# Windowed attention with sinks and a maxout FFN: 32-wide TensorE tiles for the sink part, output banks by head pair, and a split last output

## The chip, the cores and the metric

The kernel runs on one core of a Trainium2 chip. The core has TensorE (PE in the profile; PEld are its weight loads), VectorE (DVE), ScalarE (ACT), GpSimd (POOL) and SyncE (SP), which here only issues DMAs. The metric is the device time of one execution in microseconds; the time of a kernel is the median of its runs.

## The reference

Attention over 4 batches, 8 heads, 768 tokens, head size 64. A token sees itself and the 127 before it, and the first four tokens of its sequence (the sinks). The result, heads side by side, goes through an FFN whose hidden layer is the maximum of three products.

```python
scores = scale * np.matmul(q, k.transpose(0, 1, 3, 2))
is_sink = pos[None, :] < 4
in_window = (rel >= 0) & (rel < 128)              # rel = query position - key position
a = softmax(np.where(is_sink | in_window, scores, -1e9))
x = np.matmul(a, v)                               # -> (B*S, H*D) = (3072, 512)
h = np.maximum(np.maximum(x @ w1, x @ w2), x @ w3)    # d_ff = 768
return h @ w_out                                  # (3072, 512), float32
```

## The kernel before

Work is cut into 12 chunks of 256 tokens (`NCH`), three to a batch (`CPB`). In the first chunk of a batch (0, 3, 6, 9) the sinks are ordinary keys of the chunk's own blocks. In the other eight (1, 2, 4, 5, 7, 8, 10, 11) the sinks lie in front of the window and have matmuls of their own. A chunk has two halves of 128 tokens (`t`), and its heads come in four pairs (`p`, `NP`), 128 rows of d for each pair.

The order is written out by hand: `manual_schedule` keeps each engine in the order of the program, and strings such as `"Fa3 Ab00 Fa4"` list the steps. The first letter is the step, the second the chunk (a, b, c ... are given with the call), the rest its argument:

- K, Q: transposes of k and q on TensorE (`prep`, the first four chunks); D: the same by a DMA transpose on SP (`turn`), and E copies k into its place (`place_k`).
- L loads q, k and v of a chunk on SP's queue; `cast` turns them into bf16, mostly on POOL.
- S: window scores, two matmuls with 64 rows each per pair, and their exponentials on ACT (L271, L277); B only opens the banks. M: the mask, a product on DVE (L284).
- Z: sink scores (`sink_score`, L290), four matmuls that add up in one bank, and one exponential into `e_sink` (L295). Row 8·s + head of that bank holds the score of sink s for the head; `ks` carries the four sink keys, spread over a wide zeroed tile so that each pair's weights hit its own rows. X (`sink_k`, L240) fills `ks` by four copies of 64x8, on DVE (on ACT for batch 0).
- A: attention times values (`av`), arguments g (heads 0 to 3 or 4 to 7) and t. A bank holds four heads of 64 + 1 columns, the last being the sum of the weights. With sinks, the first matmul multiplies `e_sink` with `vs` (L304, 260 columns), then eight window matmuls of 65 columns are added (L312). DVE takes the reciprocals (L317) and scales into `x_sb` (L320). `vs` holds the sink values spread over 32 rows by head; it is zeroed on ACT (L117) and filled by `sink_v`, a product and a copy on POOL per batch (L172, L176).
- T: x is turned, on TensorE for the first chunks (L335, copies L337), by DMA transposes on SP from chunk 5 on (L329).
- F: one of nine hidden products (`ffn_h`, argument n = 3·fp + wi): eight matmuls of 256 columns (L350), then a copy by ACT for the first weight (L354) or a maximum by DVE (L356).
- Y, W: the output product (L370), a copy by ACT (L380) and the stores on SP (L361). For the last chunk, `ffn_y` takes half 0 as a whole (copied by DVE, L377) and `ffn_y_end` takes half 1 as two column halves (L390, L392), with stores on SP and ACT.

All of TensorE's outputs take turns in one pool of eight PSUM banks. In the loop, round i works on F and W of chunk i, A and T of chunk i+1, Z and S of chunk i+2, and turns, casts and loads ahead of them:

```python
text = "Fa0 Fa1 {} Fa2 {} Zc Sc0123 Mc0123 Wa0"
text = text.format("Ec", "Ab00 Fa3 Xb Ab01 Fa4 Ab10 Fa5 Ab11 Tb0 Tb1 Fa6 Dd Le Fa7 Fa8")
run(text, a=i, b=i + 1, c=i + 2, d=i + 3, e=i + 4)
```

`load(2, nc.scalar)` is a gate: a one-element copy by ACT holds chunk 2's loads back until ACT has come so far. The weights w are loaded by POOL's queue (`load_w`), between POOL's casts.

Of the kernel before, what the change touches and what calls it, by code (L numbers as in the profile page):

```python
# [16 lines left out]
def kernel(  # L17
# [13 lines left out]
    nc = tc.nc  # L31
# [19 lines left out]
    with tc.manual_schedule():  # L51
# [53 lines left out]
        ks = [const.tile([128, NP * 130], BF16, name=f"ks{i}") for i in range(2)]  # L105
        vs = const.tile([128, B, H, D + 1], BF16, name="vs")
# [10 lines left out]
        nc.scalar.copy(vs.rearrange("p b h d -> p (b h d)"), zc.to_broadcast([128, B * H * (D + 1)]))  # L117
# [45 lines left out]
        bm = const.tile([R, H], F32, name="bm")  # L163

        def sink_v_init():
            nc.gpsimd.memset(bm, 0.0)
            for x in range(n_sink):
                nc.gpsimd.affine_select(out=bm, in_=bm, compare_op=ALU.not_equal, fill=1.0,
                                        base=-H * x, pattern=[[-1, H]], channel_multiplier=1)

        def sink_v(b):
            nc.gpsimd.tensor_tensor(  # L172
                out=vs[0:R, b, :, 0:D],
                in0=vs_raw[:, b].unsqueeze(1).to_broadcast([R, H, D]),
                in1=bm.unsqueeze(2).to_broadcast([R, H, D]), op=ALU.mult)
            nc.gpsimd.tensor_copy(vs[0:R, b, :, D:D + 1], bm.unsqueeze(2))  # L176
# [58 lines left out]
        def sink_k(b, copy=nc.vector.tensor_copy):  # L235
            kv = ks[b % 2].rearrange("p (a y) -> p a y", y=130)[:, :, 0:8 * n_sink]
            for h in range(2):
                hp = slice(64 * h, 64 * h + 64)
                for i in range(2):
                    copy(  # L240
                        kv[hp].rearrange("p a (t i x) -> p i a t x", i=2, x=8)[:, i, :, :, h],
                        kk[b * CPB % (2 * CPB)][hp, :, 64 * i:64 * i + n_sink // 2])
# [43 lines left out]
        def sink_score(ci):  # L286
            b, c = divmod(ci, CPB)
            st = psum.tile([128, 256], F32, tag="f", name="sk")
            for p in range(NP):
                nc.tensor.matmul(st, lhsT=ks[b % 2][:, p * 128:(p + 1) * 128],  # L290
                                 rhs=qT[ci % (2 * CPB)][:, :, p].rearrange(
                                     "p i (n t) -> p n i t", n=2),
                                 start=(p == 0), stop=(p == NP - 1))
# [6 lines left out]
        def av(ci, g, t):  # L300
            b, c = divmod(ci, CPB)
            o = psum.tile([128, 4, D + 1], F32, tag="f", name="o_ps")
            if c > 0:
                nc.tensor.matmul(o, lhsT=es[ci, "sink"][:, t * 128:(t + 1) * 128],  # L304
                                 rhs=vs[:, b, 4 * g:4 * g + 4, :], start=True, stop=False,
                                 skip_group_check=True)
            for hh in range(4):
                p, h = divmod(4 * g + hh, 2)
                blocks = [(sl, n) for sl, n in ((2 * t, 2 * c + t - 1), (2 * t + 1, 2 * c + t))
                          if n >= 0]  # L310
                for x, (sl, n) in enumerate(blocks):
                    nc.tensor.matmul(o[:, hh], lhsT=es[ci, p][:, h, sl],  # L312
                                     rhs=ve[b % 2][:, n, 2 * p + h],
                                     start=(c == 0 and x == 0), stop=(x == len(blocks) - 1),
                                     skip_group_check=True)
            rc = work.tile([128, 4], F32, tag="rc", bufs=4, name="rc")
            nc.vector.reciprocal(rc, o[:, :, D])  # L317
            if g == 0:
                xs[ci, t] = work.tile([128, H, D], BF16, tag="x", bufs=4, name="x_sb")
            nc.vector.tensor_mul(xs[ci, t][:, 4 * g:4 * g + 4], o[:, :, 0:D],  # L320
                                 rc.unsqueeze(2).to_broadcast([128, 4, D]))
# [3 lines left out]
        def xpose(ci, t):  # L325
            if t == 0:
                xTs[ci] = work.tile([128, 2, DS, 128], BF16, tag="xT", bufs=3, name="xT")
            if ci > CPB + 1:
                nc.sync.dma_start_transpose(  # L329
                    out=xTs[ci][:, t], in_=xs.pop((ci, t)).rearrange("p h d -> p (h d)"))  # L330
                return
            pt = psum.tile([128, DS, 128], BF16, tag="f", name="xt_ps")
            x = xs.pop((ci, t)).rearrange("p h d -> p (h d)")
# [24 lines left out]
        def store(y, ci, t, engs=(nc.sync, nc.sync)):  # L358
            dst = out[ci * 256:ci * 256 + 256].rearrange("(t p i) m -> i p t m", t=2, i=2)
            for i in range(2):  # L360
                engs[i].dma_start(out=dst[i, :, t], in_=y[64 * i:64 * i + 64, t])  # L361

        def ffn_y(ci, ts, fbs):
# [8 lines left out]
            for t in ts:  # L372
# [3 lines left out]
                if ci == NCH - 1:  # L376
                    nc.vector.tensor_copy(y[:, t], yps.pop((ci, t)))  # L377
                    store(y, ci, t, engs=(nc.sync, nc.scalar))
                    continue
# [4 lines left out]
        def ffn_y_end(ci):  # L384

            for x in range(2):
                cols = slice(256 * x, 256 * x + 256)
                yp = psum.tile([128, 256], F32, tag="f", name="y_ps")
                for fb in range(FB):
                    nc.tensor.matmul(yp, lhsT=hs[ci][:, fb, 128:256], rhs=wo[:, fb, cols],  # L390
                                     start=(fb == 0), stop=(fb == FB - 1))
                (nc.vector.tensor_copy if x else nc.scalar.copy)(ys[ci][:, 1, cols], yp)  # L392
            store(ys[ci], ci, 1, engs=(nc.sync, nc.scalar))

        def step(op):
# [21 lines left out]
            elif name == "X":  # L417
                if ci % CPB == 0:
                    sink_k(ci // CPB)
            elif name == "A":  # L420
                av(ci, int(arg[0]), int(arg[1]))
# [6 lines left out]
            elif name == "W" and ci == NCH - 1:  # L428
                ffn_y(ci, [0], [range(FB)])
# [31 lines left out]
        sink_k(0, nc.scalar.copy)  # L461
# [3 lines left out]
        sink_v(0)  # L465
# [86 lines left out]
```

## Time and profile before

| what | value |
|---|---|
| median of 4 runs | 185.04 us (184.26 to 186.27) |
| the profiled execution | 185.58 us, of which the span in the trace is 183.8 us |
| TensorE | 173.4 us busy (94%), weight loads 136.6 us |
| VectorE, ScalarE, GpSimd | 118.0, 91.7 and 70.7 us busy |
| granted TensorE clock | 1.00 |
| hidden products L350 | 864 matmuls, 103.1 us |
| output products L370 | 138 matmuls, 32.5 us |
| sink scores L290; sink AV L304 | 32 matmuls, 4.8 us; 32 matmuls, 8.8 us |

A duration in the table of groups is that of one instruction from its start to its end. Matmuls overlap: one of 256 columns is listed with 273 ns, while one follows the next by 0.109 us. Times in the text count from the start of the span.

### The profile page before, as it was taken

How to read it: one execution, taken by the hardware profiler on the slowest of the kernel's cores; microseconds unless marked ns; L12 is line 12 of the kernel's file. 1: busy time of each engine (PE TensorE's matmuls, PEld its weight loads, DVE VectorE, ACT ScalarE, POOL GpSimd, SP SyncE). 2: the span in 40 equal slices, each digit the busy share in tenths (PEclk: the TensorE clock that was granted, in tenths of full speed). 3: DMA queues.
4: the chain of work that ended last, by engine and by line, in shares of the span. 5: the costliest groups of instructions: out<-in, count | busy, mean ns of one | idle time of the engine just before them, and what ended most of it. 6: DMA issues, size and time to landing. Idle time of an engine off the chain costs nothing.

```text
span 183.8 us, 4649 instructions
## 1 busy us (share of the span) xinstructions
PE 173.4 (94%) x1849; PEld 136.6 (74%) x1849; DVE 118.0 (64%) x257; ACT 91.7 (50%) x186; POOL 70.7 (38%) x122
## 2 busy tenths in 40 slices
PE   6987899999998899999999999999999999999990
PEld 6754889876695599589598698697796796896870
DVE  2593526787499189487769686686596785673450
ACT  6388461664941781961832923924716726622210
POOL 7476106838993565355045127145064000000000
PEclk9999999999999999999999999999999999999999
DMA  5999979999868989892687799995996632132404
GB/s 148 290 229 239 212 155 286 161 316 298 253 178 248 193 238 269 214 280 80 145 251 239 162 283 224 230 294 132 152 360 142 89 102 45 41 101 33 116 0 114
DMA packets 68021, 34.67 MB, mean 189 GB/s; under 512 B 26144, under 2 KB 64800, under 8 KB 68000
## 3 DMA queue, kind: packets, MB, share of 16 engines
q1 hardware_dynamic: 64784, 30.45, 64.6%
q0 software_dynamic: 3056, 3.67, 11.5%
q8 instruction: 14, 0.23, 0.5%
q10 hardware_dynamic: 160, 0.26, 0.4%
q14 instruction: 7, 0.06, 0.1%
HBM read 25.20 MB, written 6.29 MB: 171 GB/s over the span
## 4 chain that ended last, share of the span: by engine, by line
PE 79%; DMA 8%; DVE 5%; POOL 1%; ACT 1%; issue 1%; SPq 1%; ACTq 0%; DVEq 0%
PE h_ps L350 48%; PE y_ps L370 16%; DMA v_raw<-in_v_dram 8%; PE o_ps L312 5%; PE st L271 4%; DVE h_sb L356 3%; PE o_ps L304 2%; PE sk L290 2%; DVE x_sb L320 1%; SPq L70 1%; PE xt_ps L335 1%; POOL ve L197 1%; PE pt L218 1%; DVE rc L317 0%; POOL w L150 0%
## 5 line engine op out<-in xcount | busy, mean ns | idle before, releaser
L350 PE MATMUL h_ps<-xT,w 128*128 128x256 bf16 x864 | 103.1, 273 | 1.7 <-DMA w<-in_moe_w_dram 1.6
L350 PEld LDWEIGHTS <-w 128*128 128x128 bf16 x864 | 81.6, 98 | 13.0 <-DMA w<-in_moe_w_dram 1.9
L356 DVE TENSOR_TENSOR h_sb<-h_sb,h_ps 128x512 bf16<-128x512 bf16 x72 | 49.1, 685 | 25.9 <-PE h_ps L350 20.5
L188 POOL CAST qk_bf<-qk_raw 128x512 bf16<-128x512 f32 x42 | 28.3, 684 | 52.9 <-DMA qk_raw<-in_k_dram 38.6
L277 ACT ACTIVATE e_sb<-st 128x512 bf16<-128x512 f32 (+1 forms) x96 | 45.1, 591 | 6.7 <-PE st L271 6.7
L354 ACT CAST h_sb<-h_ps 128x512 bf16<-128x512 f32 x36 | 21.8, 611 | 49.8 <-PE h_ps L350 49.8
L284 DVE TENSOR_TENSOR e_sb<-e_sb,msk 128x1024 bf16<-128x1024 bf16 (+1 forms) x40 | 28.9, 727 | 20.0 <-ACT e_sb L277 19.9
L370 PE MATMUL y_ps<-wo,h_sb 128*128 128x512 bf16 x138 | 32.5, 379 | 1.6 <-DVE h_sb L356 1.3
L197 POOL CAST ve<-v_raw 64x512 bf16<-64x512 f32 x42 | 27.0, 642 | 15.1 <-DMA v_raw<-in_v_dram 12.8
L370 PEld LDWEIGHTS <-h_sb 128*128 128x128 bf16 x138 | 12.8, 98 | 16.3 <-DVE h_sb L356 2.8
L320 DVE TENSOR_TENSOR x_sb<-o_ps,rc 128x256 bf16<-128x256 f32 x48 | 20.4, 425 | 1.7
L312 PE MATMUL o_ps<-ve,e_sb 128*128 128x65 bf16 x352 | 19.1, 193 | 0.9 <-ACT e_sb L277 0.5
L312 PEld LDWEIGHTS <-e_sb 128*128 128x128 bf16 x352 | 17.1, 97 | 2.7 <-ACT e_sb L277 1.1
L380 ACT COPY y_sb<-y_ps 128x512 f32<-128x512 f32 x22 | 12.6, 633 | 11.0 <-PE y_ps L370 10.9
L271 PE MATMUL st<-qT,kk 64*128 64x128 bf16 (+1 forms) x256 | 13.2, 237 | 0.4 <-ACT qT L221 0.3
L271 PEld LDWEIGHTS <-kk 64*128 64x128 bf16 x256 | 8.7, 94 | 5.0 <-issue 3.6
L304 PE MATMUL o_ps<-vs,e_sink 128*128 128x260 bf16 x32 | 8.8, 274 | 0.0
L317 DVE RECIPROCAL rc<-o_ps 128x4 f32<-128x4 f32 x48 | 8.4, 176 | 0.4 <-PE o_ps L312 0.2
L221 ACT COPY qT<-pt 128x512 bf16<-128x512 bf16 x6 | 3.6, 592 | 7.7 <-PE pt L218 7.7
L115 PE MATMUL warm<-ident 128*128 128x128 bf16 x43 | 5.0, 304 | 1.4 <-POOL ident masks.py:199 1.4
L295 ACT ACTIVATE e_sink<-sk 128x256 bf16<-128x256 f32 x8 | 3.2, 394 | 6.4 <-PE sk L290 6.4
L208 DVE COPY kk<-pt 128x512 bf16<-128x512 bf16 x8 | 3.4, 422 | 4.4 <-PE pt L218 4.4
(52 smaller groups left out, 81.3 us busy)
## 6 DMA issues: line engine op xcount, KB each, us to landing
qk_raw<-in_k_dram SPq DMA_DIRECT2D x24, 256.0 KB, 4.2
qk_raw<-in_q_dram SPq DMA_DIRECT2D x24, 256.0 KB, 4.0
v_raw<-in_v_dram SPq DMA_DIRECT2D x11, 512.0 KB, 5.8
out_dram<-y_sb SPq DMA_DIRECT2D x22, 256.0 KB, 4.6
w<-in_moe_w_dram POOLq DMA_DIRECT2D x2, 768.0 KB, 10.6
wo<-in_moe_w_out_dram POOLq DMA_DIRECT2D x2, 384.0 KB, 6.5
v_raw<-in_v_dram POOLq DMA_DIRECT2D x1, 512.0 KB, 10.1
w<-in_moe_w_dram POOLq DMA_DIRECT2D x1, 512.0 KB, 8.7
```

The source lines that it names most:

```text
L188: (eng.tensor_copy if eng else nc.scalar.copy)(dst.rearrange("p i (h d) -> p h i d", d=D), src)
L197: (eng.tensor_copy if eng else nc.scalar.copy)(dst[64 * i:64 * i + 64], src[64 * n:64 * n + 64, :, i])
L271: nc.tensor.matmul(st[h][:, sl], lhsT=kx[r, p, k0:k0 + 128], rhs=qx[r], start=ci >= 2, stop=True, skip_group_check=ci < 2)
L277: nc.scalar.activation(e[:, h, lo:], st[:, lo:], AF.Exp, scale=scale)
L284: nc.vector.tensor_tensor(out=e, in0=e, in1=m, op=ALU.mult)
L312: nc.tensor.matmul(o[:, hh], lhsT=es[ci, p][:, h, sl], rhs=ve[b % 2][:, n, 2 * p + h], start=(c == 0 and x == 0), stop=(x == len(blocks) - 1),
L320: nc.vector.tensor_mul(xs[ci, t][:, 4 * g:4 * g + 4], o[:, :, 0:D], rc.unsqueeze(2).to_broadcast([128, 4, D]))
L350: nc.tensor.matmul(hp[:, f], lhsT=w_sb[wi, 2 * fp + f][:, ds], rhs=xTs[ci][:, :, ds], start=(ds == 0), stop=(ds == DS - 1))
L354: nc.scalar.copy(dst, hp)
L356: nc.vector.tensor_max(dst, dst, hp)
L370: nc.tensor.matmul(yps[ci, t], lhsT=hs[ci][:, fb, t * 128:(t + 1) * 128], rhs=wo[:, fb], start=(fb == 0), stop=(fb == FB - 1))
L380: nc.scalar.copy(y[:, t], yps.pop((ci, t)))
```

## The change

The sink scores use four tiles of 32 weight columns: pair p writes partitions 32p to 32p + 31 of the same bank, and nothing is added up. `ks` shrinks to 32 columns a pair. The sink part of AV becomes a step of its own (V, `sink_av`): it opens four banks, one for each pair with both token halves, and fills them with eight matmuls of 32 rows and 130 columns. A then works by pair (`av(ci, p)`), and x of a chunk is one tile with both halves. `vs` is made by two matmuls with a selection matrix `sel` and two copies by DVE (`sink_v`, once for all batches); POOL's products are gone, and ACT casts the raw sink values (`v_sink`). `sink_k` runs on ACT always. The last chunk's output is taken in four quarters of 128 tokens x 256 columns; the stores go out on POOL and ACT (half 0) and on SP and ACT (half 1, by column halves). In the first chunks the order of F, A and T changes.

```diff
-        ks = [const.tile([128, NP * 130], BF16, name=f"ks{i}") for i in range(2)]
-        vs = const.tile([128, B, H, D + 1], BF16, name="vs")
+        ks = [const.tile([128, NP, 32], BF16, name=f"ks{i}") for i in range(2)]
+        vs = const.tile([128, B, 2, D + 1], BF16, name="vs")
...
-        nc.scalar.copy(vs.rearrange("p b h d -> p (b h d)"), zc.to_broadcast([128, B * H * (D + 1)]))
...
+        sel = const.tile([R, 2, NP, 32], BF16, name="sel")
+        v_sink = const.tile([R, B, D + 1], BF16, name="v_sink")
         def sink_v_init():
...
+            nc.gpsimd.memset(sel, 0.0)
+            nc.gpsimd.memset(v_sink[:, :, D:D + 1], 1.0)
+            idv = ident[0:R, 0:R].rearrange("r (s p h) -> r p s h", p=NP, h=2)
+            for h in range(2):
+                nc.gpsimd.tensor_copy(sel[:, h, :, 0:2 * n_sink].rearrange(
+                    "r p (s h) -> r p s h", h=2)[:, :, :, h], idv[:, :, :, h])
+        def sink_v():
+            for h in range(2):
+                pv = psum.tile([128, B, D + 1], F32, tag="f", name="vs_ps")
+                nc.tensor.matmul(pv, lhsT=sel[:, h].rearrange("r p x -> r (p x)"), rhs=v_sink,
+                                 start=True, stop=True)
+                nc.vector.tensor_copy(vs[:, :, h], pv)
...
-        def sink_k(b, copy=nc.vector.tensor_copy):
+        def sink_k(b):
...
+                    nc.scalar.copy(
...
-                nc.tensor.matmul(st, lhsT=ks[b % 2][:, p * 128:(p + 1) * 128],
+                nc.tensor.matmul(st[32 * p:32 * p + 32], lhsT=ks[b % 2][:, p],
...
-                                 start=(p == 0), stop=(p == NP - 1))
+                                 start=True, stop=True)
...
+        def sink_av(ci):
+            b = ci // CPB
+            for p in range(NP):
+                ops[ci, p] = psum.tile([128, 2, 2, D + 1], F32, tag="f", name="o_ps")
+            for t in range(2):
+                for p in range(NP):
+                    r = slice(32 * p, 32 * p + 32)
+                    nc.tensor.matmul(ops[ci, p][:, t], lhsT=es[ci, "sink"][r, t * 128:(t + 1) * 128],
+                                     rhs=vs[r, b], start=(t == 0), stop=False,
+                                     skip_group_check=True)
...
-        def av(ci, g, t):
+        def av(ci, p):
...
+            o = ops.pop((ci, p)) if c > 0 else psum.tile([128, 2, 2, D + 1], F32, tag="f", name="o_ps")
+            for t in range(2):
...
+                for h in range(2):
+                    for x, (sl, n) in enumerate(blocks):
+                        nc.tensor.matmul(o[:, t, h], lhsT=es[ci, p][:, h, sl],
...
+            nc.vector.tensor_mul(xs[ci][:, :, 2 * p:2 * p + 2], o[:, :, :, 0:D],
+                                 rc.unsqueeze(3).to_broadcast([128, 2, 2, D]))
...
         def ffn_y_end(ci):
...
+            for q in quarters[:2]:
+                matmuls(q, range(4))
+            for q in quarters:
+                t, x = q
+                matmuls(q, range(0 if t else 4, FB))
                 cols = slice(256 * x, 256 * x + 256)
...
+                copy = nc.scalar.copy if q == (0, 1) else nc.vector.tensor_copy
+                copy(y[:, t, cols], yp[q])
+                if t == 1:
+                    store(y, ci, t, (nc.sync, nc.scalar), cols)
+                elif x == 1:
+                    store(y, ci, t, (nc.gpsimd, nc.scalar))
...
-        sink_k(0, nc.scalar.copy)
+        nc.scalar.copy(v_sink[:, :, 0:D], vs_raw)
+        sink_k(0)
...
-        sink_v(0)
...
         run("Sb23 Zb Fa0", a=0, b=1)
+        sink_v()
...
-        run("Fa3 Ab00 Ab10 Ab01 Ab11 Fa6 Tb0 Tb1 Fa1", a=0, b=1)
+        run("Fa3 Fa6 Vb Ab0 Ab1 Ab2 Ab3", a=0, b=1)
         load(2, nc.scalar)
+        run("Fa1 Fa4 Tb0 Tb1 Fa7", a=0, b=1)
...
-        for b in range(1, B):
-            sink_v(b)
...
-        run("Fb5 Sc23 Mc23 Ac00 Fb8 Ac01 Ya0 Ya1", a=0, b=1, c=2)
+        run("Fb5 Sc23 Mc23 Vc Ac0 Fb8 Ac1 Ya0 Ya1", a=0, b=1, c=2)
...
-                text = text.format("Ec", "Ab00 Fa3 Xb Ab01 Fa4 Ab10 Fa5 Ab11 Tb0 Tb1 Fa6 Dd Le Fa7 Fa8")
+                text = text.format("Ec", "Vb Ab0 Fa3 Xb Ab1 Fa4 Ab2 Fa5 Ab3 Tb0 Tb1 Fa6 Dd Le Fa7 Fa8")
```

## The prediction, made before the changed kernel was run

> **What bounds the kernel now.** I read four views in this order: the page's busy shares, the table of stages, the trace around one scoring block, and the chain of waits where TensorE (PE) has a hole. The page first:
>
> ```profile
> PE 173.4 (94%) x1849; PEld 136.6 (74%) x1849; DVE 118.0 (64%) x257; ACT 91.7 (50%) x186; POOL 70.7 (38%) x122
> ```
>
> PE is busy 94% of the span. A share is an average, so the stages (start:end, length, then busy of PE, PEld, DVE, ACT, POOL, granted clock, DMA share, GB/s):
>
> ```profile
> 18.66:47.80 29.14, 28.74 (x316) 22.88 (x316) 17.68 (x38) 14.26 (x29) 15.50 (x25) 1.00 1.02 245
> 47.80:60.30 12.50, 10.86 (x119) 8.70 (x117) 10.87 (x24) 5.46 (x13) 9.19 (x15) 1.00 0.78 215
> 88.80:166.40 77.60, 77.45 (x826) 61.54 (x826) 54.97 (x120) 38.99 (x81) 19.77 (x32) 1.00 0.72 176
> ```
>
> From 88.8 to 166.4 PE leaves 0.15 us of 77.6 empty: a microsecond taken off PE there is a microsecond of time. The only hole after the start lies in 47.8 to 60.3 (10.86 of 12.50). The chain of waits names its cause:
>
> ```profile
> 55.92 0.24 DVE ks L240 x2
> 56.17 0.26 DVE ks L240 x2
> ...
> 59.55 0.70 DVE h_sb L356
> 60.25 0.05 issue
> 60.29 0.61 PE y_ps L370 x2
> ```
>
> y of chunk 2 waits 1.5 us for the last maximum of h: DVE is behind, with the four sink-key copies (0.5 us) among its work.
>
> **Sink scores (Z).** Now four 128x128 matmuls of 256 columns; after, four of 32 weight columns, each with its own 32 output partitions. The trace around chunk 8 (PE, then its weight loads):
>
> ```profile
> 99.94 0.60 PE L290 MATMUL sk<-qT,ks 128*128 128x256 bf16 x4
> 100.48 1.06 PE L271 MATMUL st<-qT,kk 64*128 64x128 bf16 x24
> ...
> 100.47 0.83 PEld L271 LDWEIGHTS <-kk 64*128 64x128 bf16 x24 [0.21 <-issue]
> 101.46 0.62 PEld L370 LDWEIGHTS <-h_sb 128*128 128x128 bf16 x4 [0.16 <-issue]
> ```
>
> The sink matmuls follow at 0.109 us. The first 64-row one starts 0.205 after the last, so entering another tile shape costs 0.10; leaving it costs 0.09 where nothing else waits (35.03 to 35.18). Inside, two 64-row matmuls in different rows start 3 ns apart: 24 of them with 4096 columns start within 0.84 us, about half of 4096/256 x 0.109.
>
> Four concurrent 32-column tiles: 0.10 in, 0.11 of streaming, 0.01 of issue, then 0.10 into 64-row scores as today: 0.22 against 0.44, saving **0.22**. Who is late next? The first y matmul after the scores (101.55) takes the bank of the first exponential, and ACT does e_sink first: that chain (last sink start 100.27, plus 1.28) moves with the sink scores, so the saving passes. Not everywhere: in chunks 4 and 5 (i = 2, 3) ACT is behind with a y or two xT copies when Z ends (e_sink at 63.17 directly behind a y copy), and the next PE work waits for ACT's first exponential whatever Z takes: 0. Chunk 1's is hidden by the w load (PE idle 16.80 to 18.66). So 4 x 0.22 = **-0.9** (chunks 7, 8, 10, 11).
>
> Here a rule speaks against the change. The Trainium skill, TensorE: Matmul & The Clock Gate, Part 3, says that a weight load overlaps running matmuls only when their row groups differ; four column tiles share all rows. By the rule, load and stream alternate: 4 x (0.098 + 0.109) + 0.10 = 0.93, a loss of 0.49 a chunk. The row says otherwise for full tiles, which share all rows too: four loads (98 ns each) begin at 99.84, four matmuls still follow at 0.109. No row shows 32-column tiles. Ends: +0.49 and -0.33 (no switch cost); I take -0.22, nearest the row.
>
> **Sink AV (V).** Now four matmuls of 260 columns at 0.110 per chunk inside the full-array stream. After: eight 32-row matmuls of 130, four side by side: 2 x 0.055 + 0.02 + 0.10 in + 0.09 out = 0.32, saving 0.11. TensorEngine Tiling (Array Packing), Key Properties, says that a change of tiling mode drains TensorE; it would make V lose if a drain were the 0.21 that a weight load stood idle: 0.42 + 0.13 = 0.55, +0.11. The measured net prices above exclude the idle time that streaming fills, so I take them. Serial tiles would give 8 x 0.055 + 0.19 = 0.63, +0.19; no price for switching, -0.31. Six chunks (4, 5, 7, 8, 10, 11): **-0.65**.
>
> V also takes four PSUM banks at once. In the steady loop these are those of the last scores and of y's first half, free 1 us before V. In chunk 2 they are not. There V waits for the maximum after Fb2 and for the first exponential of the second score pair:
>
> ```profile
> 37.22 0.69 DVE L284 TENSOR_TENSOR e_sb<-e_sb,msk 128x1024 bf16<-128x1024 bf16 x1 [0.29 <-ACT e_sb L277]
> 37.83 1.88 DVE L356 TENSOR_TENSOR h_sb<-h_sb,h_ps 128x512 bf16<-128x512 bf16 x3
> ```
>
> The second of the three maxima ends at 39.11, the exponential at 39.43, V would come at 38.8: a stall of about 0.5, against Z's 0.13 and V's 0.11 saved, and part of the later o_ps work was waiting anyway: net **+0.15**. Behind V on PE stand A and Fb8; all wait.
>
> **By pair and the transposes.** A keeps 48 reciprocals (176 ns) and 48 products (425 ns); only their strides change: 0. But token half 0 is now complete only after the fourth A. SP's transpose T0 moves from 163.58 to about 164.7 in the last round, T1 by 1.1 too. SP has 1 to 2.5 us idle per round before T0, so the transposes, loads and stores queued behind it only slide. The landings: T1 landed 2 to 3 us before its h matmul in most rounds, but at 168.03 against 168.96 in the last. With 1.1 later that one stalls: **+0.15** (0 to 1.2 if T1 takes the 3.98 that T0 took).
>
> **Sink keys to ACT.** Twelve copies leave DVE; twelve of about 0.22 us come on ACT, queued before the third h copy, where ACT idles 2.64 us: hidden. On DVE they sit in the hole: -0.5. Also POOL loses three sink_v (1.25 us each, 45.9 to 49.2), so its casts of chunk 4 run earlier. The first mask took 1.52 us beside that product, the others 0.96 beside casts, against 0.56 with POOL idle (88.92): I take 0.6 more. The hole is 1.7 with the shorter wait before it: **-1.1** (ends -0.5, -1.7).
>
> **Start.** Order becomes Fa0, two vs matmuls, Fa3, Fa6, V, A, Fa1, Fa4, T, Fa7. Before: holes of 0.40 (v_raw), 0.28 (T for x_sb), 0.20 (xT copy). After: vs matmuls cost 0.42 with switches; their two DVE copies (0.43) delay the v casts to 21.9, but Fa6 now stands ahead of A (22.0), so nothing waits; x is ready at 24.67, T comes at 24.75 behind Fa4. Six F, A and T end at 26.08, where Fb0 starts; before, the same point was 26.66: **-0.6**. It hangs on w1's second load (landed 23.82; Fa4 wants it at 23.87). POOL without sink_v(0) issues it 1.1 us earlier, but its queue was running already; chunk 2's loads, gated earlier by ACT's order (22.7, not 25.1), compete. Ends: -0.9, +0.4. ACT's removed vs fill (1.92 us) was hidden before 6.78; its v_sink copy delays a chain that ends before w lands: 0.
>
> **Last y.** The same 6144 columns in 24 matmuls of 0.109:
>
> ```profile
> 178.04 1.47 PE L390 MATMUL y_ps<-wo,h_sb 128*128 128x256 bf16 x12
> 179.56 0.42 DVE L392 COPY y_sb<-y_ps 128x256 f32<-128x256 f32 x1 [0.62 <-PE y_ps L390]
> 180.09 0.51 ACTq L361 DMA_DIRECT2D out_dram<-y_sb  x1
> ```
>
> PE ends at 179.3 either way; the final quarter's copy still takes 0.42, its stores still leave near 180.0 and land about 2.4 (SP) and 2.7 (ACT) later. Earlier quarters leave sooner, off the path. POOL's store leaves at 178.75; a POOL issue takes 0.75 to 0.93, so only above 4 us would it be last. **-0.1** (ends -0.4, +0.8).
>
> **Sum.** -0.9 - 0.65 + 0.15 + 0.15 - 1.1 - 0.6 - 0.1 = -3.05. The profiled execution took 185.58 (span 183.8 and 1.8 around it), so 182.5; it is 0.54 above the median 185.04, so against the median **182.0**.
>
> **Rivals.**
> Serial tiles: 32-wide tiles don't run beside each other. Z +0.49 in chunks 2, 7, 8, 10, 11 (2.45), V +0.19 in seven (1.3) plus 0.2 at the start: +4.0; the rest still gives -1.65: 187.4. It decides from 0.5 us more a chunk. For it: the rule on row groups, and no row with 32. Against: the 64-row pairs 3 ns apart.
> Switches eat it: tiles run together, but drains are dearer; Z and V save nothing, and the start waits for w1: hole -1.1, rest +0.1: 184.1. For it: the 0.21 and 0.16 of idle loads at every switch.
> Late transposes: T slides past its slack; 1.2 in the last round and 0.3 in four others turn the sum into -0.8: 184.2. For it: last-round slack 0.93. Against: 2 us elsewhere.
>
> **Numbers.** Forecast 0.60; switches 0.15; late transposes 0.10; serial tiles 0.15. Faster by over 1% (what a measurement here tells from no change) 0.58, within 0.26, slower 0.16. The forecast's own ends give 180.8 to 183.6; the range reaches past the two middle cases to 185.8.
>
> **What would show it.** Right: sink scores and sink AV with starts a few ns apart; Z to first score 0.2; y's wait at 58.6 under 0.7; no gap before Fa4; a gap near 0.5 before chunk 2's sink AV. Wrong: sink starts 0.1 apart or more, gaps above 0.2 on both sides of V, a DMA wait ahead of an h matmul, POOL's store landing last.

## The result: faster by about 1 us, where 3 were forecast

The changed kernel takes 183.64 us (median of 42 runs, 182.52 to 185.69), the kernel before 184.98 in the same series (63 runs, 183.36 to 189.25). The ratio is 0.9945, 95% interval 0.9928 to 0.9961: about 1.0 us less, not the forecast 3.0. The ratio compares the fast executions of both kernels alone, so it gives less than the 1.3 us between the two medians. The profiled execution took 184.47 us with a span of 182.7, against 185.58 and 183.8.

Four segments of the span say where the difference of the two profiles, 1.16 us, lies. "Round i" is the loop's round; it begins with the first h product of chunk i.

| segment (us) | before | after | difference |
|---|---|---|---|
| start to the first h product (w lands) | 18.66 | 18.13 | -0.53 |
| first h product to round 4 | 59.62 | 58.51 | -1.11 |
| rounds 4 to 10 | 90.52 | 90.66 | +0.14 |
| round 11 to the end | 15.05 | 15.39 | +0.34 |

The first difference is no effect of the change: it ends when w lands, and over seventeen profiles of all kernels here that was anywhere from 16.9 to 18.7. The forecast had -1.7 in the second segment, -1.3 in the third and -0.1 in the last.

### The profile page after: what moved, and what is told of

It is laid out like the page before. It is cut to its first block, busy times and chain, and to the rows that moved or that the text cites. A ratio compares the mean times of both kernels' runs of the same rounds, so it can differ in the third digit from the quotient of the medians.

```text
span 182.7 us, 4713 instructions
## 1 busy us (share of the span) xinstructions
PE 170.4 (93%) x1889; PEld 130.9 (72%) x1889; DVE 118.8 (65%) x248; ACT 92.0 (50%) x198; POOL 69.0 (38%) x114
## 4 chain that ended last, share of the span: by engine, by line
PE 74%; DMA 11%; DVE 5%; ACT 4%; issue 2%; SPq 1%; POOL 0%; DVEq 0%; ACTq 0%
PE h_ps L364 47%; PE y_ps L385 14%; PE o_ps L326 6%; DMA w<-in_moe_w_dram 5%; DMA v_raw<-in_v_dram 3%; DVE h_sb L370 3%; DMA xT<-x_sb 3%; PE st L274 2%; ACT e_sb L280 2%; PE y_ps L404 1%; PE o_ps L313 1%; SPq L70 1%; PE xt_ps L349 1%; PE pt L221 1%; PE sk L293 1%
## 5 line engine op out<-in xcount | busy, mean ns | idle before, releaser
L191 POOL CAST qk_bf<-qk_raw 128x512 bf16<-128x512 f32 x42 | 27.0, 652 | 53.6 <-DMA qk_raw<-in_k_dram 42.8
L287 DVE TENSOR_TENSOR e_sb<-e_sb,msk 128x1024 bf16<-128x1024 bf16 (+1 forms) x40 | 30.7, 779 | 17.3 <-ACT e_sb L280 16.8
L200 POOL CAST ve<-v_raw 64x512 bf16<-64x512 f32 x42 | 30.8, 734 | 18.3 <-DMA v_raw<-in_v_dram 14.5
L385 PE MATMUL y_ps<-wo,h_sb 128*128 128x512 bf16 x132 | 30.8, 379 | 0.7 <-DVE h_sb L370 0.4
L326 PE MATMUL o_ps<-ve,e_sb 128*128 128x65 bf16 x352 | 17.8, 193 | 1.5 <-ACT ve L200 1.0
L326 PEld LDWEIGHTS <-e_sb 128*128 128x128 bf16 x352 | 15.8, 97 | 3.4 <-issue 1.2
L391 ACT COPY y_sb<-y_ps 128x512 f32<-128x512 f32 x22 | 12.6, 632 | 10.3 <-PE y_ps L385 10.1
L375 POOL DMA_DIRECT2D out_dram<-y_sb x1 | 0.6, 571 | 36.1 <-ACT y_sb L415 36.1
L351 ACT COPY xT<-xt_ps 128x512 bf16<-128x512 bf16 x8 | 4.3, 593 | 4.4 <-PE xt_ps L349 4.4
L116 PE MATMUL warm<-ident 128*128 128x128 bf16 x43 | 4.4, 286 | 1.4 <-POOL ident masks.py:199 1.4
```

The lines of the kernel that those rows point to most:

```text
L191: (eng.tensor_copy if eng else nc.scalar.copy)(dst.rearrange("p i (h d) -> p h i d", d=D), src)
L200: (eng.tensor_copy if eng else nc.scalar.copy)(dst[64 * i:64 * i + 64], src[64 * n:64 * n + 64, :, i])
L287: nc.vector.tensor_tensor(out=e, in0=e, in1=m, op=ALU.mult)
L326: nc.tensor.matmul(o[:, t, h], lhsT=es[ci, p][:, h, sl], rhs=ve[b % 2][:, n, 2 * p + h], start=(c == 0 and x == 0), stop=(x == len(blocks) ...
L385: nc.tensor.matmul(yps[ci, t], lhsT=hs[ci][:, fb, t * 128:(t + 1) * 128], rhs=wo[:, fb], start=(fb == 0), stop=(fb == FB - 1))
L391: nc.scalar.copy(y[:, t], yps.pop((ci, t)))
```

## The profile after, read against the one before

The page's busy line, and the table of the same three stages (start:end, length, busy of PE, PEld, DVE, ACT, POOL, clock, DMA share, GB/s):

```profile
PE 170.4 (93%) x1889; PEld 130.9 (72%) x1889; DVE 118.8 (65%) x248; ACT 92.0 (50%) x198; POOL 69.0 (38%) x114
```

```profile
18.13:47.28 29.15, 28.94 (x326) 21.92 (x326) 17.63 (x40) 15.05 (x30) 14.16 (x24) 1.00 1.13 249
47.28:58.60 11.32, 10.63 (x120) 8.71 (x117) 9.74 (x20) 6.02 (x17) 5.56 (x9) 1.00 0.94 221
87.15:164.75 77.60, 76.07 (x841) 58.62 (x840) 54.74 (x112) 40.18 (x88) 23.33 (x32) 1.00 0.82 176
```

TensorE is busy 3.0 us less in all. The middle stage lost its hole: 0.69 us are empty where 1.64 were. But in the last stage 1.53 us of 77.6 are empty where 0.15 were. TensorE was relieved, and part of the relief came back as waiting.

**Tiles run beside each other.** The timeline around the sink scores of chunk 8 (start, duration, engine, operation):

```profile
98.28 0.10 PEld L293 LDWEIGHTS <-ks 128*32 128x32 bf16 x4 [0.21 <-issue]
98.28 0.29 PE L293 MATMUL sk<-qT,ks 128*32 128x256 bf16 x4
98.50 0.83 PEld L274 LDWEIGHTS <-kk 64*128 64x128 bf16 x24
...
98.62 0.38 ACT L298 ACTIVATE e_sink<-sk 128x256 bf16<-128x256 f32 x1 [1.40 <-PE sk L293]
```

All four loads fit in 0.10 us, the four matmuls start 3 to 4 ns apart, and the first score follows 0.22 after the first sink matmul. The chain of waits shows the sink AV of chunk 8, and the window matmuls behind it:

```profile
118.15 0.22 PE o_ps L313 x8
118.38 0.35 PE o_ps L326 x8
```

Before, the four sink matmuls took 0.11 per bank inside a stream at 0.24 for each bank's eight window matmuls; now 0.22 for the sinks and 0.11 on the first window bank for leaving the tile shape: 0.33 for what took 0.44.

**The old hole.** The chain ahead of y of chunk 2:

```profile
57.85 0.70 DVE h_sb L370
58.55 0.04 issue
58.59 0.61 PE y_ps L385 x2
```

The copies into `ks` are gone from this chain, and the last maximum ends 0.57 us after TensorE is ready for it, not 1.50.

**The new hole.** The chain of waits at the start of round 8:

```profile
123.83 0.78 SPq L343
124.61 0.04 issue
124.65 4.96 DMA xT<-x_sb
129.61 0.14 issue
129.75 1.25 PE h_ps L364 x10
```

The x transpose of the second half leaves at 124.65 and lands 4.96 us later; TensorE had finished y at 128.11 and stands for 1.42 us. Round 7 as a whole, before and after (two tables of stages, one line of each):

```profile
117.61:130.68 13.07, 13.00 (x138) 10.12 (x137) 9.43 (x21) 6.75 (x16) 4.92 (x8) 1.00 0.83 218
```

```profile
115.37:129.75 14.38, 13.05 (x142) 9.69 (x140) 10.76 (x21) 7.59 (x17) 6.80 (x10) 1.00 1.16 210
```

The DMA engines, at a share of 0.83 of the round before, are at 1.16 (a packet counts from its start to its end, so waiting packets can bring it over 1). SP's queue shows how it got there. Before, in the order of time, around the start of round 7 at 117.61:

```profile
110.79 2.53 SPq L329 DMA_TRANSPOSE xT<-x_sb  x2
...
116.08 0.58 SPq L70 DMA_DIRECT2D qk_raw<-in_k_dram  x1
...
119.39 2.33 SPq L361 DMA_DIRECT2D out_dram<-y_sb  x2
```

and after, around its start at 115.37:

```profile
110.13 3.12 SPq L343 DMA_TRANSPOSE xT<-x_sb  x2
...
116.12 1.43 SPq L70 DMA_DIRECT2D qk_raw<-in_k_dram  x1
...
120.15 2.28 SPq L375 DMA_DIRECT2D out_dram<-y_sb  x2
```

Before, a chunk's loads leave 1.5 us ahead of the round's first h product and the stores 1.8 behind it. The last store lands at +8.3, 1.7 after x is transposed again at +6.6. After, the transposes leave at +7.9, the loads behind them at +0.8 and the stores at +4.8; the last store lands at +11.05, 3.15 after the next transposes have left. The transpose's own landing follows that of the store. In rounds 5 to 8 of all seventeen profiles (68 rounds) the first x transpose landed 0.4 to 0.9 us after the round's last store in 56, and 1.3 to 2.8 after it in the other 12. In rounds 9 and 10, where no loads are left and the stores have landed before it leaves, it took about 2.5 us in 29 cases of 34 and 2.7 to 4.0 in the other five. In the round above it landed 2.0 after the last store; a standstill, described with s65, came between.

## The experiments

Ratios are to the kernel before, timed on the same chip in the same series; their intervals are 0.3 to 0.7% wide on either side, so an effect of half a microsecond shows in the segments of the profile rather than in the median.

**c_after: the changed kernel again**, as the yardstick of the first series.

> The changed kernel again, on the chip of the next three. Theory (late transposes): it is 0.3 to 0.8% below the kernel before, ratio 0.992 to 0.997, and in its profile the two transposes of x land 4 us or more after their issue in several rounds from 88 us on, with a hole of TensorE ahead of some round's first hidden product. Rival (a chance event of one execution): the transposes land after about 2.5 us here and there is no hole.

Measured: 0.988 (0.9816 to 0.9945). Its profile has the hole at the start of round 8 too, but 0.46 us long; another wait shows at 22.6 to 23.3 (see st_old). The loss is real and its size changes from execution to execution.

**e_early: transposes 0.9 us earlier.**

```diff
-"Vb Ab0 Fa3 Xb Ab1 Fa4 Ab2 Fa5 Ab3 Tb0 Tb1 Fa6 Dd Le Fa7 Fa8"
+"Vb Ab0 Fa3 Xb Ab1 Ab2 Fa4 Ab3 Tb0 Tb1 Fa5 Fa6 Dd Le Fa7 Fa8"
```

> The changed kernel, but in the loop the third A stands directly behind the second and the fourth one hidden product earlier (Vb Ab0 Fa3 Xb Ab1 Ab2 Fa4 Ab3 Tb0 Tb1 Fa5 Fa6), so x is complete about one hidden product (0.87 us) earlier. Theory (transposes that leave late meet the loads and stores of the round): they leave 0.9 us earlier, land within 3 us, the hole is gone, and the kernel is 0.7 to 1.6 us faster than the changed one. Rival (the transposes have slack, the missing microseconds are lost at the start and the end): within 0.3 us of the changed kernel, or slower because VectorE has two products of x one behind the other.

Measured: 0.9843 (0.9784 to 0.9902), 0.6 us under the yardstick in the median, which the intervals don't resolve; rounds 4 to 10 take 89.21 us, with no wait for a transpose. Transposes still landed up to 5.3 us after leaving, but in time. So 89.21 is what these rounds take when nothing is late: 1.31 under before.

**b_late: the kernel before with its transposes exchanged**, so that the first leaves as late as after the change.

```diff
-"Ab00 Fa3 Xb Ab01 Fa4 Ab10 Fa5 Ab11 Tb0 Tb1 Fa6 Dd Le Fa7 Fa8"
+"Ab00 Fa3 Xb Ab01 Fa4 Ab10 Fa5 Ab11 Tb1 Tb0 Fa6 Dd Le Fa7 Fa8"
```

> The kernel before, with the two transposes of x issued in the other order in the loop (half 1, which is complete last, first), so both leave as late as in the changed kernel and nothing else differs. Theory: loads and stores slide with them, the transposes land after 4 us or more in some rounds, and the kernel loses 0.5 to 1.6 us, most of it as a hole ahead of a round's first hidden product. Rival (SyncE's idle time takes the shift up): within 0.3 us of the kernel before, landings stay near 2.5 us, at most a stall of 0.2 us in the last round.

Measured: 1.0017 (0.9973 to 1.0061), no hole; only the last round is longer, by 0.14. In the kernel before, this much lateness is absorbed: the transposes landed after 2.4 to 3.1 us, but for one of round 9 that took 4.0. In rounds 5 to 8 the last store landed 1.9 to 2.4 us after they left (before 1.1 to 3.3; after the change 3.15 to 4.1). Its rounds are 0.1 to 0.3 longer, which would leave loads and stores that time; that is argued, not shown. Leaving late is not enough by itself.

**e_oldtail: the last y as before**, all else changed (`ffn_y` for half 0, two column halves for half 1, stores on SP and ACT).

> The changed kernel with the last chunk's output as in the kernel before (half 0 whole, half 1 in two column halves, stores of whole rows on SyncE and ScalarE). Theory (stores of 1 KB rows land later: 3.0 and 3.2 us against 2.4 and 2.7): 0.2 to 0.5 us faster than the changed kernel, last stores landing 2.4 to 2.7 us after issue. Rival (the split helps as meant): 0.1 to 0.4 us slower.

Measured: 0.9905 (0.9865 to 0.9945). The median can't tell it from the changed kernel, and this profile has holes of 0.58 and 1.15 us at the start of rounds 8 and 9. The end can: the last store lands 14.05 us after the first h product of round 11; before 14.03, after 14.40. Of the issues, with the time to landing, the kernel before

```profile
out_dram<-y_sb SPq DMA_DIRECT2D x2, 128.0 KB, 2.3
out_dram<-y_sb ACTq DMA_DIRECT2D x2, 128.0 KB, 2.7
```

and the changed kernel:

```profile
out_dram<-y_sb ACTq DMA_DIRECT2D x1, 128.0 KB, 2.4
out_dram<-y_sb POOLq DMA_DIRECT2D x1, 128.0 KB, 2.5
out_dram<-y_sb SPq DMA_DIRECT2D x2, 64.0 KB
out_dram<-y_sb ACTq DMA_DIRECT2D x2, 64.0 KB, 3.0
```

The last stores are half as large (1 KB instead of 2 KB of a row) and leave 0.07 us earlier, but land about 3.0 and 3.2 us later: 0.36 lost. The split alone does not explain it. Of the twelve profiles with the split, ten have the last landing at 14.32 to 14.41, and in each an 8 KB packet of another instruction queue came 12.8 to 12.9 us after the first h product of round 11, among these stores. In the other two, st_old and dve_keys, no such packet came there, and the last store landed at 13.63 and 13.67, about 0.4 ahead of the kernel before. The list of DMA queues from 174 us to the end has this line in the changed kernel and none of this queue in dve_keys:

```profile
q14 instruction: 1, 0.01, 0.1%
```

and in dve_keys the last stores on ACT land earlier than the 3.0 above:

```profile
out_dram<-y_sb ACTq DMA_DIRECT2D x2, 64.0 KB, 2.7
```

That the packet delays them is a tie of ten against two, not a test: no run moved it by itself.

**e_fullz: sink scores on the whole array again** (and `ks` wide and zeroed again, which the cut leaves out).

```diff
-nc.tensor.matmul(st[32 * p:32 * p + 32], lhsT=ks[b % 2][:, p], ...  start=True, stop=True)
+nc.tensor.matmul(st, lhsT=ks[b % 2][:, p * 128:(p + 1) * 128], ...  start=(p == 0), stop=(p == NP - 1))
```

> The changed kernel with the sink scores on the whole array again: per chunk four accumulating matmuls with 128 weight columns (zero but for the pair's 32) in place of four 32-column ones. TensorE executes as many instructions, so the transfers come at the same places. Tiles run side by side (my theory): sink scores take 0.44 instead of 0.22 us; by the round-to-round differences +0.16 (chunks 7, 10) and +0.22 (chunks 8, 11), 0.76 in all, of which the hole ahead of a first h product (0.5 to 1.4) gives back a part, as the transposes gain that much time: +0.2 to +0.8 us, ratio 0.989 to 0.998. If the tiles were worth nothing: within 0.1 us of the changed kernel.

Measured: 0.9973 (0.9939 to 1.0006). The chain shows 0.45 us again:

```profile
98.08 0.45 PE sk L293 x4
98.53 0.02 issue
98.55 0.39 ACT e_sink L298
```

Rounds 5, 6, 8 and 9 are longer than the undisturbed ones by 0.22, 0.21, 0.21 and 0.22: the tiles of the scores are worth 0.86 us. One hole of 0.33 us is left.

**s65 and s15: idle matmuls at the start.** The trace's packets show that transposes at times stand still, all at once, for 1 to 3 us, and mostly when a 16 KB packet of the profile's "instruction" queue has come. The Trainium skill (Runtime: NRT & Kernel Launch, Terms) says that an engine's instruction memory is refilled in 16 KiB blocks; here such a packet comes about every 120 matmuls (84 to 181 in the traces), each with its weight load. In the changed kernel, by the table of stages:

```profile
126.00:127.00 1.00, 1.00 (x6) 0.44 (x5) 0.79 (x2) 1.00 (x4) 0.94 (x2) 1.00 2.51 144
127.00:128.00 1.00, 1.00 (x6) 0.49 (x5) 0.91 (x2) 1.00 (x4) 0.96 (x2) 1.00 0.07 6
```

The last column is GB/s: 6 from 127 to 128, with the x transposes in flight, after a 16 KB packet at 126.20. Idle matmuls ahead of the first h product (65 and 15 of them) are meant to move these packets in all later rounds and nothing else:

```diff
+def dummies(tile, n):
+    for _ in range(n):
+        nc.tensor.matmul(tile[:, 0:64], lhsT=ident, rhs=ident[:, 0:64], start=True, stop=True)
```

> The changed kernel with 65 idle matmuls of 64 columns added at the start (22 behind the third warm-up, 43 ahead of the first h product, where TensorE waits for v and for the first w load anyway). Nothing else moves, except that TensorE's instruction stream is 130 instructions further on in every later stage, so that the 16 KB instruction transfers (one on every 120 or so matmuls) come some 5 us earlier in each round, among the plain loads instead of among the transposes. Theory A (a transpose that is in flight when such a transfer comes stands still for about 1.4 us; that is what made the x transposes of rounds 7 to 9 land after 4 to 5 us): no frozen transpose from round 4 on, x transposes land within 3.5 us, the hole ahead of a first h product is under 0.2 us, ratio to the kernel before 0.982 to 0.986 (after: 0.988 and 0.9945), 0.4 to 1.0 us under the changed kernel. Theory B (the transposes are late only because they queue behind loads and stores that now run later): holes stay at 0.4 to 1.5 us in the same rounds, ratio 0.988 to 0.9945.

> The changed kernel with 15 such idle matmuls only. The transfers move by about 1 us and still meet transposes in four or five rounds (by the trace of the changed kernel the x transposes of rounds 5 to 8). Theory A: freezes stay, holes of 0.4 to 2 us in all ahead of first h products, ratio 0.988 to 0.997, no better than the changed kernel. Theory B, or a gain from the idle matmuls as such (a warmer start): the same as with 65.

Measured: s65 0.9919 (0.9883 to 0.9956), s15 0.9934 (0.989 to 0.9977): not to be told apart in the median, so the expected 0.982 to 0.986 failed. In the profile the two differ. s65 has no standstill after 60 us and one hole of 0.30 us; the same seconds of its round 7:

```profile
126.00:127.00 1.00, 1.00 (x6) 0.49 (x5) 0.79 (x2) 1.00 (x4) 0.94 (x2) 1.00 0.75 147
127.00:128.00 1.00, 1.00 (x7) 0.42 (x5) 0.91 (x2) 1.00 (x4) 0.90 (x3) 1.00 0.87 149
```

s15 has three standstills behind such a packet and two without one, and holes of 0.25 and 0.85. But in s65 the transposes of rounds 5 to 8 still landed 2.9 to 4.9 us after leaving: without any standstill they land behind the stores, the first of each round 0.5 to 0.6 after the last store. Nor did every packet stop a transpose: at 98.59 and 111.20 one came in s65 between an x transpose's leaving and its landing, and nothing stood still.

**e_early_s65: both.**

> The changed kernel with the second and third AV pairs back to back, so that the transposes leave 1 us earlier in the steady rounds, and with the 65 idle matmuls. Theory A and B together: e_early had no hole left, so the shift can add little: ratio 0.982 to 0.986, within 0.3 us of e_early (0.9843) and of the shifted kernel without it. If the two were separate losses that add, 0.978 to 0.981.

Measured: 0.9946 (0.9911 to 0.998), a miss. Its profile, of the slowest of its twelve executions, has a hole of 0.93 us at the start of round 6, behind a standstill from 100.2 to 103.1 in which a 16 KB packet came at 101.38, and a wait of 1.43 us for w1 at the start. The round's last store landed 6.0 us after the first transpose had left, and that transpose 0.5 later. Early by 0.9 us is not early enough for such a case.

**s70 and s5: the packets moved once more.**

> The changed kernel with 70 idle matmuls at the start. Looked at is the profile from round 4 on, not the time. Theory A (transfers freeze transposes): from round 5 on no transfer meets a transpose, no group of transpose packets stands still for over 0.9 us, and the holes ahead of first h products in rounds 5 to 10 sum to under 0.35 us. Theory B (late departure alone): the transposes still land 4 to 5 us after leaving and the holes sum to 0.5 to 1.7 us, as in the unshifted profiles.

> The changed kernel with 5 idle matmuls: by its trace the transfers meet transposes in the six rounds from 4 to 9. Theory A: four or more groups of frozen packets, holes ahead of first h products of 0.5 to 2 us in all. Theory B: holes as in any other profile of this order, 0.3 to 1.7 us; it can't be told from A by this run alone, only if the freezes are missing where the transfers meet transposes, which would refute A.

Measured, in one profile each: s70 has a hole of 1.56 us, where under 0.35 was expected. Its chain, and three lines of its stages:

```profile
99.00 5.21 DMA xT<-x_sb
104.22 0.14 issue
104.35 1.69 PE h_ps L371 x14
```

```profile
100.00:101.00 1.00, 0.87 (x7) 0.48 (x5) 0.32 (x1) 1.00 (x3) 0.61 (x1) 1.00 4.22 147
101.00:102.00 1.00, 1.00 (x7) 0.46 (x5) 0.85 (x2) 1.00 (x4) 0.95 (x1) 1.00 0.41 34
102.00:103.00 1.00, 0.96 (x5) 0.23 (x3) 0.89 (x2) 1.00 (x4) 0.95 (x1) 1.00 0.10 13
```

A packet came at 101.24, among the transposes, and here is the only standstill and the only hole; the rounds after it have neither. The packets were moved, then, but not where I meant. And the slowing began at 100.5, before the packet: the packet did not begin it here, and may at most have lengthened it. s5 has three standstills and a hole of 0.43. Over all seventeen profiles, 41 of 49 standstills (ten or more transpose packets without an end for 0.8 us, after 60 us) have such a packet within them or in the 1.3 us before, and each of the eleven holes of over 0.4 us at a first h product follows a standstill. That is a strong tie, not a proof of cause; eight standstills have no such packet.

**early2: transposes as early as before**, with the old last y.

```diff
-"Vb Ab0 Fa3 Xb Ab1 Fa4 Ab2 Fa5 Ab3 Tb0 Tb1 Fa6 Dd Le Fa7 Fa8"
+"Vb Ab0 Fa3 Xb Ab1 Ab2 Ab3 Tb0 Tb1 Fa4 Fa5 Fa6 Dd Le Fa7 Fa8"
```

> The changed kernel with all of the last three AV pairs back to back in the steady rounds, so that the transposes leave at about 6 us of the round (before: 6.6; changed: 7.5 to 7.9), and with the last y of the kernel before. Theory B: loads and stores move forward with them, transposes have landed before the first h product even where one is frozen, holes under 0.2 us in all, steady seven rounds 89.2 to 89.6 us, last landing 14.05 after the last first h product, ratio 0.984 to 0.990. Rival: AV runs into the masks (VectorE) of its fourth pair, and TensorE waits there 0.2 to 0.5 us in each of seven rounds: ratio 0.992 to 1.000.

Measured: 0.9885 (0.9828 to 0.9943), 182.97 us. Rounds 4 to 10 take 89.21, the last store lands at 14.05. SP's queue in round 6 (start at 101.81) and round 7 (114.95):

```profile
108.12 2.56 SPq L343 DMA_TRANSPOSE xT<-x_sb  x2
...
113.46 0.57 SPq L70 DMA_DIRECT2D qk_raw<-in_k_dram  x1
...
117.11 2.18 SPq L375 DMA_DIRECT2D out_dram<-y_sb  x2
```

The loads leave 1.5 ahead of the round again. One transpose took 5 us here too, but landed at +11.3 of its round, ahead of the first h product at +12.6. So an early departure left room for the late landing, in this one profile as in that of e_early; e_early_s65 is the case where it was not enough. TensorE did not wait for the masks. Its span, 180.5, is 2.2 under that of the changed kernel; the medians' intervals overlap, so it is shown faster than the kernel before, not than the changed one.

**st_old: the start in the old order; st_load2: chunk 2's loads later.**

```diff
 # st_old
-run("Fa3 Fa6 Vb Ab0 Ab1 Ab2 Ab3"); load(2, nc.scalar); run("Fa1 Fa4 Tb0 Tb1 Fa7")
+run("Fa3 Vb Ab0 Ab1 Ab2 Ab3 Fa6 Tb0 Tb1 Fa1"); load(2, nc.scalar)    # Fa4 Fa7 behind Fb1
 # st_load2
-load(2, nc.scalar); run("Fa1 Fa4 Tb0 Tb1 Fa7")
+run("Fa1 Fa4 Tb0 Tb1 Fa7"); load(2, nc.scalar)
```

> The changed kernel with the start order of the kernel before (third h product, AV, sixth, transposes, first of the second weight; chunk 2's loads behind them; the fourth and seventh h products of chunk 0 behind those of chunk 1). My theory: the new order puts the fourth h product of chunk 0 right where the second part of w1 lands, which depends on what the DMA engines have moved and not on when TensorE starts; in the profiles so far of the new order this wait was 0 to 1.6 us and the stretch from the first h product to round 4 took 58.0 to 59.7 (mean 58.7; before 59.6 twice). With the old order that wait is gone and the stretch takes about 58.9 whatever the loads do: 0.2 above the mean of the new order, within 0.3 us of the changed kernel in the median, ratio 0.993 to 0.998. The prediction's theory (order worth 0.6): 0.4 to 0.7 us slower than the changed kernel, ratio 0.997 to 0.999.

> The changed kernel with chunk 2's loads gated behind the seventh h product of chunk 0 instead of ahead of the first of the second weight: they leave at about 25.5 instead of 22 us. If these loads take bandwidth from w1's second part (theory A), it lands 0.3 to 0.8 us earlier in the executions where it is late, the wait ahead of the fourth h product stays under 0.3, and the stretch to round 4 takes 58.0 to 58.4: ratio 0.990 to 0.993. If w1's second part is late by what was queued before it (w0, v, w1's first part, theory B), nothing changes: wait 0 to 1.6, ratio 0.9945 as for the changed kernel.

Measured: st_old 0.9889 (0.9836 to 0.9942), its stretch to round 4 is 59.26; st_load2 0.992 (0.9879 to 0.9962), stretch 58.55. What the new order risks shows in the chain of s15:

```profile
15.02 9.07 DMA w<-in_moe_w_dram
24.08 0.05 issue
24.13 1.05 PE h_ps L369 x8
```

TensorE stands 1.63 us for the second part of w1. In twelve profiles of the new order with the loads in their place, this wait was under 0.2 in seven and 0.3, 0.7, 0.7, 1.4 and 1.6 in five, and the stretch 58.0 to 59.7, mean 58.63. In st_load2 and best the wait is gone, but chunk 2's k transposes then wait 0.33 and 0.51 for their casts. Two profiles can't settle that loads take w1's bandwidth; the old order, by one profile, is 0.6 slower than the mean of the new one, with its own holes of 0.32, 0.28 and 0.49. My expectation for its ratio failed; the last store's landing, 0.4 ahead of the kernel before instead of 0.36 behind it (see e_oldtail), is 0.8 us of it in the profile.

**dve_keys: sink keys on DVE again** for chunks 3, 6 and 9.

```diff
-nc.scalar.copy(
+copy(          # nc.vector.tensor_copy
```

> The changed kernel with the sink keys of chunks 3, 6 and 9 copied by VectorE again (chunk 0's stay on ScalarE, as they were). My theory: the four copies, some 0.5 us, stand in the only hole that VectorE makes, ahead of y of chunk 2: it is 0.3 to 0.6 in the profiles of the changed kernel and 1.5 in that of before, and comes out at 0.8 to 1.1: 0.5 us slower than the changed kernel, ratio 0.996 to 0.998. Rival: the hole shrank because POOL lost its sink products and chunk 4's casts and the masks ran earlier: hole stays under 0.6, same time as the changed kernel.

Measured: 0.9855 (0.9809 to 0.9901), outside what I expected and not resolved from the changed kernel. The last store lands 0.7 us earlier than in the changed kernel (see e_oldtail), which the expectation did not foresee. The hole in the profile behaves as expected, 0.86 us against 0.57; the last maximum now ends at 58.75 for a TensorE that was ready at 57.94:

```profile
58.05 0.70 DVE h_sb L370
58.75 0.05 issue
58.80 0.61 PE y_ps L385 x2
```

The other profiles with the keys on ACT and chunk 2's loads in their place have 0.28 to 0.72 here (mean 0.42), so by this one profile the keys are 0.1 to 0.6 of the 1.2 us. The rest would be POOL's three sink products; that was not tried by itself.

**best: e_early, the old last y and st_load2 together.**

> The changed kernel with three edits: transposes 1 us earlier in the steady rounds (second and third AV pairs back to back), the last y as in the kernel before, chunk 2's loads behind the seventh h product. By my sum of segments: steady rounds 89.2 instead of 89.7 to 90.7, last landing 0.35 earlier, start 58.0 to 58.4: 1.0 us below the changed kernel, ratio 0.985 to 0.989. If the execution decides by where the 16 KB transfers fall and the early transposes only move the collision: 0.991 to 0.994.

Measured: 0.9891 (0.9835 to 0.9947). The segments came as summed (stretch 58.21, rounds 89.36, last landing 14.04), the ratio a little above the range.

## Why the prediction was wrong, step by step

The size failed, not the direction. To keep one lucky or unlucky execution from deciding, the steps are set against means over the profiles that share the part in question:

| step | predicted | found | from |
|---|---|---|---|
| sink scores | -0.9 | -0.86 | e_fullz, round by round |
| sink AV | -0.65 | -0.45 | undisturbed rounds (e_early): -1.31, less the scores; not tried by itself |
| chunk 2 | +0.15 | +0.30 | profile |
| late transposes | +0.15 | +0.9 | rounds 4 to 10: mean 90.1 of eleven profiles with the transposes where the change put them (e_fullz less its scores), against 89.21 |
| hole of DVE | -1.1 | -1.2 | waits of y of chunk 2: 1.69 before, mean 0.47 of eleven profiles |
| start | -0.6 | -0.1 | mean stretch 58.63 against 59.62, less chunk 2 and the hole |
| last y | -0.1 | +0.37 | last landing, ten profiles alike; -0.4 in the two without the 8 KB packet |
| sum | -3.05 | -1.0 | median ratio: -1.0 |

**Late transposes: the step that failed most.** The prediction saw that both transposes leave 1.1 us later, and said that SP "has 1 to 2.5 us idle per round before T0, so the transposes, loads and stores queued behind it only slide". They slide, but into each other: the loads and stores that slide with them still land when the next transposes leave, and the first transpose lands only after the last of these stores. With the transposes where the change put them, the last store of rounds 5 to 8 landed 3.35 us after they left in the mean of eleven profiles, against 2.05 before. That a shorter round of TensorE is the reason was not shown. I priced the delay from SP's idle time and put the slide itself at nothing, though the trace of before had the meeting in it: in round 6 the last store landed 3.3 after the first transpose had left, and the transpose took 3.8. Only the last round was charged; that one had no hole in any profile, and there the transposes landed after about 2.5 us. The holes came behind rounds 5 to 8. Moving the transposes forward gave most of it back: the four profiles with early transposes (e_early, best, early2, e_early_s65) have 89.21, 89.36, 89.21 and 90.14 for these rounds. The rival "late transposes" named a delay past the slack, but in other rounds and as 2.4 us; that its total of -0.8 lies near the measured -1.0 is luck, as the start and the last y missed too. It had a chance of 0.10.

**Start.** "It hangs on w1's second load (landed 23.82; Fa4 wants it at 23.87)" was the right place, and its end of +0.4 the right warning; I took the lucky value for the likely one. In the profile of the changed kernel the start is 0.24 shorter: the three waits of 0.40, 0.28 and 0.20 are gone, the sink AV is 0.1 shorter and the two vs matmuls cost the expected 0.42, but w1 is waited for by 0.10 and the xT copy by 0.23, a wait that the sum did not have. In the mean of twelve profiles the wait for w1 is 0.43.

**Last y.** "its stores still leave near 180.0 and land about 2.4 (SP) and 2.7 (ACT) later" was the wrong term in ten profiles, 3.0 and 3.2, and came true in two: in st_old and dve_keys the last store landed 2.4 to 2.5 us after its issue. An instruction packet among the stores was no term of the sum. The stated worst case, POOL's store landing last, did not come: it landed after 2.5 us.

**Sink AV and chunk 2.** Per chunk it was 0.33, as predicted. Chunk 4 gained nothing, since its transposes wait for x; in two rounds (5 and 8, which have no sink AV, so this is a loss of the scores) 0.05 went into y's wait for the first exponential, 0.24 instead of 0.18. The stall at chunk 2 was 0.31 + 0.16, the predicted 0.5, but more of it stayed on the path. The chain there:

```profile
37.12 1.29 DVE h_sb L370 x2
38.41 0.04 issue
38.45 0.21 PE o_ps L313
```

**Right.** The tiles run side by side; the rule on row groups would have had 0.93 us for the scores and was off for these tiles, while the measured price of entering another shape (0.10 in, 0.09 out) held. The rivals "serial tiles" and "switches eat it" are out. The hole of DVE closed by what was said, though how much of it was the keys and how much POOL's products is open.

## What to carry to other kernels

When TensorE is the bound and gets shorter, ask of each DMA queue what it will run into when it starts later: here a transpose landed behind the round's last store, so the time to take was that store's landing, not the transpose's own 2.5 us. Let the transfers that close the loop leave early; here moving the AV pairs together was worth 0.9 us in rounds 4 to 10 by two profiles, as much as the tiles of the scores. A last store that is cut to start earlier gained 0.4 or lost 0.4 here, with nothing else changed in the last round, so judge it in more than one version of the kernel.

## What was not expected of the hardware

- DMA transposes in flight can stand still for 1 to 3 us, with 6 GB/s moved in a whole microsecond; 41 of 49 such standstills came with a 16 KB packet of the instruction queue, while some packets met transposes and nothing stopped (s65). The cause stays open.
- The last stores landed 0.7 us later in the ten profiles in which an 8 KB instruction packet came among them than in the two in which none did.
- Where a load lands relative to the start of TensorE's work changed by 1.6 us between executions of nearly the same program, so an order that leaves it no slack has a stretch of 58.0 to 59.7 us.
- Four 32-column tiles that share all 128 rows start 3 to 4 ns apart, and their four weight loads take 0.10 us together.
